# Pairing f tiles and joining outputs with scores in the steady part of an attention and feed-forward kernel

## The chip, the cores and the metric

The kernel runs on one core of one Trainium2 chip. A core has five engines that run their own instruction queues in order and meet through semaphores: PE (TensorE, matrix products), DVE (VectorE), ACT (ScalarE), POOL (GpSimd) and SP (SyncE, which here only issues DMA transfers). PE writes its results to PSUM, which has eight banks of 128 partitions by 2 KiB. Everything else lies in SBUF. The metric is the device time of one execution in microseconds (us), as the median of several runs; less is better.

## The reference

Four batches of 768 tokens with 8 heads of 64 pass through an attention with a local window and one summary per block of 32 keys, and then through a feed-forward layer with a squared ReLU.

```python
block, window = (32, 16)
k_sum = k.reshape(B, H, nb, block, D).max(axis=3)
v_sum = v.reshape(B, H, nb, block, D).mean(axis=3)
scores_l = scale * np.matmul(q, k.transpose(0, 1, 3, 2))
mask_l = np.abs(pos[:, None] - pos[None, :]) < window
scores_s = scale * np.einsum('bhsd,bhnd->bhsn', q, k_sum) + np.log(block)
scores_all = np.concatenate([np.where(mask_l, scores_l, -1e9), scores_s], axis=-1)
a = softmax(scores_all)                      # with 1e-9 added to the sum
out = np.matmul(a, np.concatenate([v, v_sum], axis=2))
...
x = out.transpose(0, 2, 1, 3).reshape(B * S, H * D)     # 3072 x 512
h = np.maximum(x @ w_in, 0.0)                           # 3072 x 2048
return h * h @ w_out                                    # 3072 x 512
```

All arrays are 32-bit floats.

## The kernel before

The 3072 tokens are 24 token tiles of 128 (six per batch, numbered g from 0). Two token tiles make a chunk c, 12 in all; the hidden width of 2048 is 16 f tiles of 128.

The feed-forward layer works on a chunk and an f tile at a time. `ffn1(c, f)` is twelve matmuls of 128 by 128 by 256 in the reduced format float32r: four slices of the model width, each as high part of w times high part of x, low part of w times high part of x, and high part of w times low part of x. They collect in one PSUM bank, `ph`; there are three such banks. `squares(ph)` then makes h squared in two parts: ACT takes the ReLU `r` and its square `gh` (the high part), DVE multiplies `ph` by `r` in place and subtracts `gh` to get `gl` (the low part). That subtraction is the last reader of the bank. `ffn2` is six matmuls of 128 by 128 by 512 per f tile (two token tiles times gh with the high part of w, gh with the low part, gl with the high part). They collect over all 16 f tiles in the two `o_ps` banks, which `evict` copies to SBUF and stores when the chunk's last f tile is in.

The attention of one token tile g is a list of steps on the same engines. `scores` (16 matmuls with a 64 by 64 stationary operand, in plain float32, each seen as two in the trace) writes `s_ps`; `softmax` runs, per head, a masked minimum on DVE (`mask_max`) and an exponential on ACT; `inverse` (DVE) and `norm` (POOL) divide by the sums; `turn` transposes the result in 32 by 32 blocks on DVE, in three parts of four instructions; `outputs` (16 matmuls with a 128 by 64 stationary operand, again two each in the trace) writes `x_ps`; `split_x` makes the high and low part of x on ACT and DVE. Beside these go loads (`load_qk`, `load_v`, two tiles ahead), and per batch the summaries of the next batch: `load_kv`, `sum_k`, `sum_v`, `place_k`, `place_v`. The tiles `s_ps` (two banks) and `x_ps` (one bank) have one buffer each.

The order of all work is written out by hand; no scheduler moves it. For chunks 0 and 1 (token tiles 0 to 6, with the conversion of the weights among them) it is the long list of tokens in `START`. From chunk 2 on, `slot(c, f, side, last)` issues one f tile: ffn1, then the ffn2 of the f tile two places back (`BEHIND` is 2), then the side work, then the squares, and then the work in `last`. Which attention steps go into which slot is given by `steps(g)`, two lists of eleven places, and by three calls of `at`, which set the places of tile 2c + 2 against f + 3, of tile 2c + 3 against f - 5 and of tile 2c + 4 against f - 13. Work in `side` stands on DVE and ACT ahead of that f tile's squares; work in `last` behind them, and PE work in it behind the slot's ffn2. PE therefore runs ffn1 (f), ffn2 (f - 2), ffn1 (f + 1), ffn2 (f - 1) and so on, with a tile's scores or outputs between an ffn2 and the next ffn1. The tokens in START are not that regular: there runs of two or three ffn1 stand together, and runs of ffn2, and one outputs stands directly ahead of a scores.

Of the kernel before, what the change touches and what calls it, by code (L numbers as in the profile page):

```python
# [24 lines left out]
P = 128  # L25
NT = S // P
# [3 lines left out]
NF = DF // P  # L30
NC4 = DM // P
SPARE = 1
BEHIND = 2
KPAD = S + 2 * WINDOW
NK = 96 + NB
FROM_KT = 4
# [35 lines left out]
def attn_ffn_kernel(ctx: ExitStack, tc: tile.TileContext, q, k, kt, v, vt, v0, w, masks, ident, mean, out):  # L72
# [43 lines left out]
    def load_qk(g):  # L116
        load_q(g)
        load_k(g)
# [36 lines left out]
    def load_kv(b, p):  # L155
        kv[b, p] = r = room(F32, "kv")
        nc.sync.dma_start(out=r[:, 0:S], in_=kt[b, p])
        nc.sync.dma_start(out=r[:, S : 2 * S], in_=vt[b, p])
# [12 lines left out]
    def place_k(g):  # L171
        nc.vector.tensor_copy(out=k_sb[g % 2][:, 4], in_=ksum.unsqueeze(1).to_broadcast([P, 2, NPAIR, NB]))

    def place_v(g):
        dst = v_sb[g % 2][96:128]
        if g % 2 == 0:
            for a in range(4):
                nc.vector.transpose(
                    out=dst[:, 0, :].rearrange("a (p c) -> a p c", c=128)[:, :, a * 32 : a * 32 + 32],
                    in_=vsum[a * 32 : a * 32 + 32],  # L180
                )
        else:
            nc.gpsimd.tensor_copy(out=dst[:, 0, :], in_=v_sb[0][96:128, 0, :])
        nc.gpsimd.tensor_copy(out=dst[:, 1, :], in_=v_sb[0][96:128, 0, :])
# [46 lines left out]
    def scores(g, p0, p1):  # L231


        if g not in s_ps:
            s_ps[g] = ps_s.tile([P, 2, NPAIR, P], F32, name="s_ps")
        for p in range(p0, p1):
            for r, s in ((0, 0), (1, 1), (0, 1), (1, 0)):
                rs, ss = slice(r * 64, r * 64 + 64), slice(s * 64, s * 64 + 64)
                nc.tensor.matmul(  # L239
                    s_ps[g][ss, r, p, 0:NK], lhsT=q_sb[g % 2][rs, s, p, :], rhs=k_sb[g % 2][rs, :, s, p, :],  # L240
                    start=True, stop=True,
                )
# [33 lines left out]
    def softmax(g, h0, h1):  # L276

        for h in range(h0, h1):
            mask_max(g, h)
            exponentials(h)  # L280

    def inverse(half):
        nc.vector.tensor_scalar_add(sm[half], sm[half], 1.0e-9)  # L283
        nc.vector.reciprocal(sm[half], sm[half])
        del nmx[half]

    def norm(half, eng):
        e = e_sb[:, half * 4 : half * 4 + 4, 0:NK]
        eng.tensor_mul(out=e, in0=e, in1=sm[half].unsqueeze(2).to_broadcast([P, 4, NK]))  # L289
# [8 lines left out]
    def turn(g, n0, n1):  # L298

        blocks = [(i, j) for i in range(4) for j in ((0, 1, 3) if i % 2 == 0 else (1, 2, 3))]  # L300
        for i, j in blocks[n0:n1]:
            nc.vector.transpose(  # L302
                out=pT[g % 2][j * 32 : j * 32 + 32, :, i * 32 : i * 32 + 32],
                in_=e_sb[i * 32 : i * 32 + 32, :, j * 32 : j * 32 + 32],
            )
# [35 lines left out]
    def ffn1(c, f):  # L341
        ph = ps_h.tile([P, 4, P], F32, name="ph").rearrange("p a b -> p (a b)")[:, 0:CT]
        n = 0
        for cc in range(NC4):
            for w, x in ((0, xh), (1, xh), (0, xl)):
                nc.tensor.matmul(  # L346
                    ph, lhsT=w_sb[f][:, w, cc * P : (cc + 1) * P], rhs=x[c][:, cc, :], start=(n == 0), stop=(n == 3 * NC4 - 1)
                )
                n += 1
        return ph  # L350
# [7 lines left out]
        return r  # L358

    def high_square(r):  # L360
        gh = work.tile([P, CT], F32R, name="gh", tag="gh", bufs=3)
        nc.scalar.activation(gh, r, AF.Square)  # L362
        return gh

# [2 lines left out]
        nc.vector.tensor_mul(out=ph, in0=ph, in1=r)  # L367

    def low_square(ph, gh):
        gl = work.tile([P, CT], F32R, name="gl", tag="gl", bufs=3)  # L370
        nc.vector.tensor_sub(out=gl, in0=ph, in1=gh.bitcast(F32))  # L371
        return gl

    def squares(ph):
        r = relu(ph, nc.scalar)
        gh = high_square(r)
        square(ph, r)
        return gh, low_square(ph, gh)

    def ffn2(c, f, gh, gl, first, last):  # L380
        if first:
            o_ps[c] = [ps_o.tile([P, DM], F32, name="o_ps") for _ in range(TPC)]
        for tt in range(TPC):
            ts_ = slice(tt * P, (tt + 1) * P)
            n = 0
            for g_, w in ((gh, 0), (gh, 1), (gl, 0)):
                nc.tensor.matmul(  # L387
                    o_ps[c][tt], lhsT=g_[:, ts_], rhs=w_sb[f][:, w, DM:],
                    start=(first and n == 0), stop=(last and n == 2),
                )  # L390
                n += 1

    def evict(c, f, tt, eng):

        if (c, tt) in parked:
            ob = parked[c, tt]
            nc.vector.tensor_add(out=ob, in0=o_ps[c][tt], in1=ob)
        else:
            ob = work.tile([P, DM], F32, name="ob", tag="ob", bufs=4)
            copy(eng, ob, o_ps[c][tt])  # L400
        if f < NF - 1:
            parked[c, tt] = ob
        else:
            r0 = c * CT + tt * P
            nc.sync.dma_start(out=out[r0 : r0 + P, :], in_=ob)
# [4 lines left out]
    n_c = n_g // TPC  # L410
    behind = []

    def follow(c, f, gh, gl, first, last):
        ffn2(c, f, gh, gl, first, last)
        if last:
            for tt in range(TPC):
                evict(c, f, tt, nc.scalar)

    def slot(c, f, side, last):


        ph = ffn1(c, f)
        if len(behind) == BEHIND:
            follow(*behind.pop(0))
        for do in side:
            do()
        behind.append((c, f, *squares(ph), f == 0, f == NF - 1))
        for do in last:
            do()

    def steps(g):


        b, t = divmod(g, NT)
        side, last = [[] for _ in range(11)], [[] for _ in range(11)]
        if b and t < 2:
            side[6].append(lambda: place_v(g))
        if t == NT - 1 and b + 1 < B:

            side[1].append(lambda: place_k(g + 1))  # L440
            side[2].append(lambda: place_k(g + 2))
        last[0].append(lambda: scores(g, 0, NPAIR))
        if g + 2 < n_g:
            last[0].append(lambda: load_qk(g + 2))
        side[1].append(lambda: softmax(g, 0, 2))
        side[2].append(lambda: softmax(g, 2, 5))
        side[3] += [lambda: inverse(0), lambda: norm(0, nc.gpsimd), lambda: softmax(g, 5, 8)]
        side[4] += [lambda: inverse(1), lambda: norm(1, nc.gpsimd)]
        for n in range(3):
            side[5 + n].append(lambda n=n: turn(g, 4 * n, 4 * n + 4))  # L450
        last[9].append(lambda: outputs(g))
        if g + 2 < n_g:
            last[9].append(lambda: load_v(g + 2))
        side[10].append(lambda: split_x(g))
        if b and t in (3, 4) and b + 1 < B:
            p = 2 * (t - 3)
            last[0].append(lambda: load_kv(b + 1, p))
            side[4] += [lambda: sum_k(b + 1, p), lambda: sum_v(b + 1, p)]
            last[4].append(lambda: load_kv(b + 1, p + 1))
            side[8] += [lambda: sum_k(b + 1, p + 1), lambda: sum_v(b + 1, p + 1)]  # L460
        return side, last


# [86 lines left out]
    with tc.manual_schedule(engines=None):  # L550
        for token in START.split():
            what, i, j, eng = re.fullmatch(r"(L:[a-z]+|F[12]|[A-Z]+)\.?(\d*)\.?(\d*)([avp]?)", token).groups()
            i, j = int(i or 0), int(j or 0)
            if what.startswith("L:"):
                load(what[2:], i)
            else:
                begin(what, i, j, engines.get(eng))
        tiles = {g: steps(g) for g in range(6, n_g)}

        def at(side, last, g, step):  # L560

            if g in tiles and 0 <= step < 11:
                side += tiles[g][0][step]
                last += tiles[g][1][step]

        place_k(7)
        load_q(7)
        load_k(7)
        load_v(6)
        load_v(7)  # L570
        load_qk(8)
        softmax(6, 0, 5)
        behind += [(*units[i][:2], *g_of[i], False, i == 31) for i in (30, 31)]
        for c in range(2, n_c):
            for f in range(NF):
                side, last = [], []
                at(side, last, 2 * c + 2, f + 3)
                at(side, last, 2 * c + 3, f - 5)
                at(side, last, 2 * c + 4, f - 13)
                slot(c, f, side, last)  # L580
        for p in behind:
            follow(*p)


def _masks():
# [64 lines left out]
```

## Time and profile before

| | us |
|---|---|
| median of three runs | 632.94 |
| the three runs | 632.94, 629.68, 633.24 |
| the profiled execution, whole | 633.5 |
| its span, first to last instruction | 631.7 |

The profile comes from one execution. The span is what the trace covers, and the rest of the execution's time lies around it. PE was busy for 39.58 of the first 60 us, for 80.56 of the next 82.03, and for all of the 438.54 after them up to 580.57. The mean clock granted to PE over the run was 0.992 of full speed.

How to read the lines below: "busy" of an engine is the time in which at least one of its instructions ran; PEld are PE's weight loads, which run beside its matmuls. A matmul's shown length includes its way through the array, so consecutive matmuls overlap in the listing and the distance between starts says what one costs. In the chain of waits each piece is given with its start, its length up to the next piece, and the line and count of its instructions. In a timeline, equal neighbours are put into one row with their count, and square brackets hold the engine's idle time before the row and what ended it. A row of waits gives the engine, line and tile that waited, what it waited for, and the total, the number and the longest of such waits.

### The profile page before, as it was taken

The numbers are of one execution on the slowest core, as the hardware profiler recorded it, in microseconds if no ns is written. First come the engines' busy times: TensorE is split into PE (matmuls) and PEld (weight loads), VectorE is DVE, ScalarE is ACT, GpSimd is POOL, SyncE is SP. The second block draws the span as 40 slices with busy tenths as digits, with TensorE's granted clock in tenths as the row PEclk, the third lists the DMA queues.
The fourth block names the chain that finished last, engine by engine and source line by source line (L and its number), as shares of the span: only waits on it lengthen the run. The fifth ranks groups of instructions, "written<-read, shape, count | busy, mean of one in ns | idle before, by whom it ended". The sixth has DMA issues, their size and how long they took to land.

```text
span 631.7 us, 13371 instructions
## 1 busy us (share of the span) xinstructions
PE 606.1 (96%) x5216; PEld 539.2 (85%) x5216; DVE 406.5 (64%) x1232; ACT 299.6 (47%) x855; POOL 96.3 (15%) x83
## 2 busy tenths in 40 slices
PE   2689999999999999999999999999999999999997
PEld 1588888988889889889888889898898898888996
DVE  4689789778656577665665686774773674664222
ACT  2789987334434435435435335345344344442322
POOL 2545762001101101001011011011011010010000
PEclk9969999999999999999999999999999999999999
DMA  9999510462220333212202315302102210000000
GB/s 285 371 352 324 204 67 6 141 208 74 67 69 34 118 119 132 68 23 79 67 7 96 117 51 162 106 2 85 62 23 69 76 26 26 34 2 1 34 0 34
DMA packets 19855, 60.38 MB, mean 96 GB/s; under 512 B 2768, under 2 KB 2896, under 8 KB 17744
## 3 DMA queue, kind: packets, MB, share of 16 engines
q1 hardware_dynamic: 19792, 59.53, 28.3%
q8 instruction: 41, 0.67, 0.4%
q14 instruction: 22, 0.18, 0.1%
HBM read 53.23 MB, written 6.29 MB: 94 GB/s over the span
## 4 chain that ended last, share of the span: by engine, by line
PE 91%; DMA 3%; DVE 3%; ACT 2%; SPq 0%; issue 0%; POOL 0%; DVEq 0%; POOLq 0%
PE ph L346 42%; PE o_ps L387 40%; PE x_ps L315 4%; PE s_ps L239 3%; DMA q_sb<-in_q 2%; DMA mask_sb<-in_masks 1%; DVE w_sb L225 1%; PE s_ps L254 1%; PE ph L295 1%; ACT e_sb L274 0%; PE o_ps L130 0%; ACT w_sb L107 0%; ACT w_raw L210 0%; SPq L153 0%; DVE sm L283 0%
## 5 line engine op out<-in xcount | busy, mean ns | idle before, releaser
L346 PE MATMUL ph<-xh,w_sb 128*128 128x256 f32 x1536 | 280.3, 282 | 1.0 <-DVE w_sb L225 0.7
L346 PEld LDWEIGHTS ph<-xh,w_sb 128*128 128x128 f32 x1536 | 243.5, 189 | 17.2 <-issue 3.0
L387 PE MATMUL o_ps<-w_sb,gh 128*128 128x512 f32 x768 | 238.2, 391 | 0.0
L346 PE MATMUL ph<-xl,w_sb 128*128 128x256 f32 x768 | 213.9, 278 | 0.2 <-DVE xl L332 0.2
L367 DVE TENSOR_TENSOR ph<-ph,r 128x256 f32<-128x256 f32 x192 | 82.6, 431 | 121.7 <-ACT r L355 119.1
L387 PE MATMUL o_ps<-w_sb,gl 128*128 128x512 f32 x384 | 151.4, 394 | 0.9 <-DVE gl L371 0.9
L355 ACT ACTIVATE r<-ph 128x256 f32<-128x256 f32 x180 | 68.4, 380 | 175.3 <-PE ph L346 164.9
L387 PEld LDWEIGHTS o_ps<-w_sb,gh 128*128 128x128 f32 x768 | 131.3, 188 | 18.0 <-issue 0.2
L346 PEld LDWEIGHTS ph<-xl,w_sb 128*128 128x128 f32 x768 | 145.1, 189 | 0.4 <-DVE xl L332 0.4
L274 ACT ACTIVATE e_sb<-e_sb,nmx 128x120 f32<-128x120 f32 x192 | 73.9, 386 | 86.3 <-DVE nmx L266 86.1
L289 POOL TENSOR_TENSOR e_sb<-e_sb,sm 128x480 f32<-128x480 f32 x43 | 43.4, 1010 | 416.1 <-DVE nmx L266 362.5
L371 DVE TENSOR_TENSOR gl<-ph,gh 128x256 fp32r<-128x256 f32 x192 | 81.5, 425 | 27.2 <-ACT gh L362 4.6
L302 DVE STREAM_TRANSPOSE pT<-e_sb 32x256 f32<-32x256 f32 x216 | 94.2, 436 | 4.4 <-POOL e_sb L289 0.8
L362 ACT ACTIVATE gh<-r 128x256 fp32r<-128x256 f32 x192 | 80.3, 418 | 13.4 <-DVE r L357 4.2
L387 PEld LDWEIGHTS o_ps<-w_sb,gl 128*128 128x128 f32 x384 | 72.2, 188 | 15.8 <-DVE gl L371 1.3
L266 DVE CUSTOM_DVE_ANT_0 e_sb<-s_ps,mask_sb 128x120 f32<-128x120 f32 x192 | 43.9, 275 | 13.5 <-PE s_ps L239 9.8
L218 POOL TENSOR_TENSOR w_raw<-w_raw 128x1024 int32<-128x1024 int32 x16 | 34.3, 2151 | 26.9 <-ACT w_raw L210 11.0
L332 DVE TENSOR_TENSOR xl<-x_ps,xh 128x512 fp32r<-128x512 f32 x24 | 16.6, 690 | 32.3 <-ACT xh L329 32.3
L315 PEld LDWEIGHTS x_ps<-pT,v_sb 128*64 128x64 f32 x768 | 25.3, 141 | 13.4 <-issue 12.6
L274 ACT ACTIVATION_READ_ACCUMULATOR e_sb<-e_sb,nmx 128x1 f32 x192 | 36.0, 188 | 0.0
L315 PE MATMUL x_ps<-pT,v_sb 128*64 128x64 f32 x768 | 28.6, 229 | 5.6 <-issue 5.3
L329 ACT CAST xh<-x_ps 128x512 fp32r<-128x512 f32 x24 | 14.1, 586 | 28.9 <-PE x_ps L315 28.5
(46 smaller groups left out, 292.3 us busy)
## 6 DMA issues: line engine op xcount, KB each, us to landing
w_raw<-in_w SPq DMA_DIRECT2D x16, 1024.0 KB, 14.1
v_sb<-in_v SPq DMA_DIRECT2D x24, 384.0 KB, 4.2
k_sb<-in_k SPq DMA_DIRECT2D x20, 384.0 KB, 3.9
kv<-in_kt SPq DMA_DIRECT2D x16, 384.0 KB, 3.4
q_sb<-in_q SPq DMA_DIRECT2D x24, 256.0 KB, 3.3
out<-ob SPq DMA_DIRECT2D x24, 256.0 KB, 2.1
kv<-in_vt SPq DMA_DIRECT2D x12, 384.0 KB, 4.2
vn<-in_v SPq DMA_DIRECT2D x2, 768.0 KB, 11.0
```

The source lines that it names most:

```text
L218: nc.gpsimd.tensor_tensor(out=hi, in0=hi, in1=lo, op=ALU.add)
L266: nc.vector.tensor_tensor_reduce(out=e_sb[:, h, 0:NK], in0=s_ps[g][:, h % 2, h // 2, 0:NK], in1=m, scale=-scale, scalar=3.0e38, op0=ALU.ad ...
L274: nc.scalar.activation(e, e, AF.Exp, bias=nmx[half][:, i : i + 1], scale=-1.0, accum_out=sm[half][:, i : i + 1])
L289: eng.tensor_mul(out=e, in0=e, in1=sm[half].unsqueeze(2).to_broadcast([P, 4, NK]))
L302: nc.vector.transpose(out=pT[g % 2][j * 32 : j * 32 + 32, :, i * 32 : i * 32 + 32], in_=e_sb[i * 32 : i * 32 + 32, :, j * 32 : j * 32 + 32],)
L315: nc.tensor.matmul(xp[o : o + 64, h // 2, s * 64 : s * 64 + 64], lhsT=v_sb[g % 2][:, s, h * 64 : h * 64 + 64], rhs=pT[g % 2][:, h, s * 64 ...
L346: nc.tensor.matmul(ph, lhsT=w_sb[f][:, w, cc * P : (cc + 1) * P], rhs=x[c][:, cc, :], start=(n == 0), stop=(n == 3 * NC4 - 1))
L355: nc.scalar.activation(r, ph, AF.Relu)
L362: nc.scalar.activation(gh, r, AF.Square)
L367: nc.vector.tensor_mul(out=ph, in0=ph, in1=r)
L371: nc.vector.tensor_sub(out=gl, in0=ph, in1=gh.bitcast(F32))
L387: nc.tensor.matmul(o_ps[c][tt], lhsT=g_[:, ts_], rhs=w_sb[f][:, w, DM:], start=(first and n == 0), stop=(last and n == 2),)
```

## The change

The steady part is rewritten; START, the layouts and all tile shapes stay as they are. A slot now issues two f tiles: ffn1 of both, then the ffn2 of the two f tiles of the slot before (`finish`), then for each of the two its side work and its squares, then, if a chunk ended, the evictions, and then the work in `last`. `gh` and `gl` get four buffers instead of three, in START as well. The list of steps has twelve places, two per slot: scores at place 1 and outputs at place 9. The calls of `at` set the places of tile 2c + 2 against f + 6 (f + 4 in chunk 2), of 2c + 3 against f - 2 and of 2c + 4 against f - 10, so that the outputs of a tile and the scores of the next fall in the same slot. Softmax is cut 3, 3, 2 heads instead of 2, 3, 3. The next batch's summaries are loaded and reduced one at a time in tiles 2 to 5 of a batch, instead of two each in tiles 3 and 4.

```diff
+    def finish():
+
+        for p in behind:
+            ffn2(*p)
+        done = [p[:2] for p in behind if p[-1]]
+        behind.clear()
+        return done[0] if done else None
 
     def slot(c, f, side, last):
-        ph = ffn1(c, f)
-        if len(behind) == BEHIND:
-            follow(*behind.pop(0))
-        for do in side:
-            do()
-        behind.append((c, f, *squares(ph), f == 0, f == NF - 1))
+        ph = [ffn1(c, f + i) for i in range(2)]
+        done = finish()
+        for i in range(2):
+            for do in side[i]:
+                do()
+            behind.append((c, f + i, *squares(ph[i]), f + i == 0, f + i == NF - 1))
+        for tt in range(TPC if done else 0):
+            evict(*done, tt, nc.scalar)
         for do in last:
             do()
...
-        gh = work.tile([P, CT], F32R, name="gh", tag="gh", bufs=3)
+        gh = work.tile([P, CT], F32R, name="gh", tag="gh", bufs=4)
...
-        last[0].append(lambda: scores(g, 0, NPAIR))
+        last[1].append(lambda: scores(g, 0, NPAIR))
...
-        side[1].append(lambda: softmax(g, 0, 2))
-        side[2].append(lambda: softmax(g, 2, 5))
-        side[3] += [lambda: inverse(0), lambda: norm(0, nc.gpsimd), lambda: softmax(g, 5, 8)]
-        side[4] += [lambda: inverse(1), lambda: norm(1, nc.gpsimd)]
+        side[2].append(lambda: softmax(g, 0, 3))
+        side[3].append(lambda: softmax(g, 3, 6))
+        side[4] += [lambda: inverse(0), lambda: norm(0, nc.gpsimd), lambda: softmax(g, 6, 8)]
+        side[5] += [lambda: inverse(1), lambda: norm(1, nc.gpsimd)]
         for n in range(3):
-            side[5 + n].append(lambda n=n: turn(g, 4 * n, 4 * n + 4))
+            side[6 + n].append(lambda n=n: turn(g, 4 * n, 4 * n + 4))
         last[9].append(lambda: outputs(g))
...
+        if b and t >= 2 and b + 1 < B:
+            last[1].append(lambda: load_kv(b + 1, t - 2))
+            side[4].append(lambda: sum_k(b + 1, t - 2))
+            side[5].append(lambda: sum_v(b + 1, t - 2))
...
-        softmax(6, 0, 5)
+        softmax(6, 0, 6)
...
-            for f in range(NF):
-                side, last = [], []
-                at(side, last, 2 * c + 2, f + 3)
-                at(side, last, 2 * c + 3, f - 5)
-                at(side, last, 2 * c + 4, f - 13)
+            for f in range(0, NF, 2):
+                side, last = [[], []], []
+                at(side, last, 2 * c + 2, f + (4 if c == 2 else 6))
+                at(side, last, 2 * c + 3, f - 2)
+                at(side, last, 2 * c + 4, f - 10)
                 slot(c, f, side, last)
```

On PE, the place of token tile 11's outputs in chunk 4. The names are those of the section on the kernel: `x_ps` rows are outputs, `s_ps` rows scores, `ph` rows ffn1, `o_ps` rows ffn2; 16 instructions in one row are all of one tile. Before, the following tile's scores stand one f tile earlier than these outputs:

```order
L387 MATMUL o_ps<-w_sb,gh 128x512 x2
L387 MATMUL o_ps<-w_sb,gl 128x512
L239 MATMUL s_ps<-k_sb_79,q_sb_83 64x120 x16
L346 MATMUL ph<-xh,w_sb 128x256 x2
L346 MATMUL ph<-xl,w_sb 128x256
```

and the outputs themselves:

```order
L387 MATMUL o_ps<-w_sb,gl 128x512
L315 MATMUL x_ps<-pT_87,v_sb_82 64x64 x16
L346 MATMUL ph<-xh,w_sb 128x256 x2
L346 MATMUL ph<-xl,w_sb 128x256
L346 MATMUL ph<-xh,w_sb 128x256 x2
```

In the changed kernel PE has, at the same outputs (its lines are one lower):

```order
L345 MATMUL ph<-xl,w_sb 128x256
L386 MATMUL o_ps<-w_sb,gh 128x512 x2
L386 MATMUL o_ps<-w_sb,gl 128x512
L386 MATMUL o_ps<-w_sb,gh 128x512 x2
L386 MATMUL o_ps<-w_sb,gl 128x512
L386 MATMUL o_ps<-w_sb,gh 128x512 x2
L386 MATMUL o_ps<-w_sb,gl 128x512
L386 MATMUL o_ps<-w_sb,gh 128x512 x2
L386 MATMUL o_ps<-w_sb,gl 128x512
L314 MATMUL x_ps<-pT_87,v_sb_82 64x64 x16
L238 MATMUL s_ps<-k_sb_79,q_sb_83 64x120 x16
L345 MATMUL ph<-xh,w_sb 128x256 x2
```

The ffn2 rows of two f tiles now follow each other, and the scores have moved behind the outputs with nothing between them. In the whole steady part this meeting occurs 16 times; tile 7's scores and tile 6's and 23's outputs stand alone.

On ACT, one tile's softmax with the split of the tile before it. Here `e_sb` rows are the exponentials of so many heads, `r` and `gh` the squares of one f tile, `xh` the split. Before:

```order
L274 ACTIVATE e_sb,sm<-e_sb,nmx 128x120 x2
L355 ACTIVATE r<-ph 128x256
L362 ACTIVATE gh<-r 128x256
L329 CAST xh<-x_ps 128x4x128
L274 ACTIVATE e_sb,sm<-e_sb,nmx 128x120 x3
L355 ACTIVATE r<-ph 128x256
L362 ACTIVATE gh<-r 128x256
L274 ACTIVATE e_sb,sm<-e_sb,nmx 128x120 x3
```

In the changed kernel:

```order
L328 CAST xh<-x_ps 128x4x128
L273 ACTIVATE e_sb,sm<-e_sb,nmx 128x120 x3
L354 ACTIVATE r<-ph 128x256
L361 ACTIVATE gh<-r 128x256
L273 ACTIVATE e_sb,sm<-e_sb,nmx 128x120 x3
L354 ACTIVATE r<-ph 128x256
L361 ACTIVATE gh<-r 128x256
L273 ACTIVATE e_sb,sm<-e_sb,nmx 128x120 x2
```

The split has moved ahead of all of the tile's exponentials. The first six heads and two squares now belong to one slot, the last two heads to the next.

More of the change, by code (lines that the diff above doesn't have):

```diff
@@ L32 @@
 SPARE = 1
-BEHIND = 2
 KPAD = S + 2 * WINDOW
@@ L369, in low_square @@
     def low_square(ph, gh):
-        gl = work.tile([P, CT], F32R, name="gl", tag="gl", bufs=3)
+        gl = work.tile([P, CT], F32R, name="gl", tag="gl", bufs=4)
         nc.vector.tensor_sub(out=gl, in0=ph, in1=gh.bitcast(F32))
@@ L411, in attn_ffn_kernel @@
     behind = []
[L413 to L417, printed above, removed]
-    def slot(c, f, side, last):
-        ph = ffn1(c, f)
-        if len(behind) == BEHIND:
-            follow(*behind.pop(0))
-        for do in side:
-            do()
-        behind.append((c, f, *squares(ph), f == 0, f == NF - 1))
+    def finish():
[4 more added lines that the diff above has]
+        return done[0] if done else None
+    def slot(c, f, side, last):
+        ph = [ffn1(c, f + i) for i in range(2)]
[6 more added lines that the diff above has]
+            evict(*done, tt, nc.scalar)
         for do in last:
@@ L434, in steps @@
         b, t = divmod(g, NT)
-        side, last = [[] for _ in range(11)], [[] for _ in range(11)]
+        side, last = [[] for _ in range(12)], [[] for _ in range(12)]
+        last[1].append(lambda: scores(g, 0, NPAIR))
+        if g + 2 < n_g:
+            last[1].append(lambda: load_qk(g + 2))
         if b and t < 2:
[L437 to L441, printed above, removed]
-        last[0].append(lambda: scores(g, 0, NPAIR))
-        if g + 2 < n_g:
-            last[0].append(lambda: load_qk(g + 2))
-        side[1].append(lambda: softmax(g, 0, 2))
-        side[2].append(lambda: softmax(g, 2, 5))
-        side[3] += [lambda: inverse(0), lambda: norm(0, nc.gpsimd), lambda: softmax(g, 5, 8)]
-        side[4] += [lambda: inverse(1), lambda: norm(1, nc.gpsimd)]
+            side[7].append(lambda: place_v(g))
+        side[2].append(lambda: softmax(g, 0, 3))
+        side[3].append(lambda: softmax(g, 3, 6))
+        side[4] += [lambda: inverse(0), lambda: norm(0, nc.gpsimd), lambda: softmax(g, 6, 8)]
+        side[5] += [lambda: inverse(1), lambda: norm(1, nc.gpsimd)]
         for n in range(3):
-            side[5 + n].append(lambda n=n: turn(g, 4 * n, 4 * n + 4))
+            side[6 + n].append(lambda n=n: turn(g, 4 * n, 4 * n + 4))
         last[9].append(lambda: outputs(g))
@@ L454, in steps @@
         side[10].append(lambda: split_x(g))
[L455 to L460, printed above, removed]
+        if b and t >= 2 and b + 1 < B:
+            last[1].append(lambda: load_kv(b + 1, t - 2))
+            side[4].append(lambda: sum_k(b + 1, t - 2))
+            side[5].append(lambda: sum_v(b + 1, t - 2))
+        if t == NT - 1 and b + 1 < B:
+            side[5] += [lambda: place_k(g + 1), lambda: place_k(g + 2)]
         return side, last
@@ L560, in at @@
         def at(side, last, g, step):
-            if g in tiles and 0 <= step < 11:
-                side += tiles[g][0][step]
-                last += tiles[g][1][step]
+            for i in range(2):
+                if g in tiles and 0 <= step + i < 12:
+                    side[i] += tiles[g][0][step + i]
+                    last += tiles[g][1][step + i]
         place_k(7)
@@ L571, in attn_ffn_kernel @@
         load_qk(8)
-        softmax(6, 0, 5)
+        softmax(6, 0, 6)
         behind += [(*units[i][:2], *g_of[i], False, i == 31) for i in (30, 31)]
         for c in range(2, n_c):
-            for f in range(NF):
-                side, last = [], []
-                at(side, last, 2 * c + 2, f + 3)
-                at(side, last, 2 * c + 3, f - 5)
-                at(side, last, 2 * c + 4, f - 13)
+            for f in range(0, NF, 2):
[3 more added lines that the diff above has]
+                at(side, last, 2 * c + 4, f - 10)
                 slot(c, f, side, last)
-        for p in behind:
-            follow(*p)
+        done = finish()
+        for tt in range(TPC):
+            evict(*done, tt, nc.scalar)
 def _masks():
```

## The prediction

> **What bounds the kernel now.** Short names: F1 and F2 are the twelve and six matmuls of one f tile (ffn1, ffn2), S and O the scores and outputs of one token tile, a chunk two token tiles. I read the head of the page first, then the busy times by stretch, the chain of waits, and the timelines of the engines. The page's engine line and the row for the stretch from the first F2 of chunk 2 to 580.57 us (PE, weight loads, DVE, ACT, POOL, with instruction counts; then clock, DMA share, GB/s):
>
> ```profile
> span 631.7 us, 13371 instructions
> PE 606.1 (96%) x5216; PEld 539.2 (85%) x5216; DVE 406.5 (64%) x1232; ACT 299.6 (47%) x855; POOL 96.3 (15%) x83
> 142.03:580.57 438.54, 438.54 (x3701) 389.68 (x3700) 285.77 (x913) 189.35 (x606) 40.86 (x45) 1.00 0.20 65
> ```
>
> In the part that is rewritten PE is busy for all of 438.54 us at full granted clock. No wait can be removed there. What can change is how tightly matmuls follow each other, and that is read off starts. The chain of waits around one S and one O (start, length to the next piece, what):
>
> ```profile
> 303.15 1.38 PE o_ps L387 x6
> 304.53 0.98 PE s_ps L239 x32
> 305.51 1.58 PE ph L346 x12
> 307.09 1.38 PE o_ps L387 x6
> 308.46 1.08 PE x_ps L315 x32
> 309.55 1.58 PE ph L346 x12
> 311.12 1.37 PE o_ps L387 x6
> 312.49 1.39 PE ph L346 x12
> ```
>
> An undisturbed f tile is 1.37 + 1.39 = 2.76 us (the last two pieces). With S it is 307.09 - 303.15 = 3.94, so S costs 1.18; with O 311.12 - 307.09 = 4.03, so O costs 1.27. Both exceed their own 0.98 and 1.08, because the F1 behind them reads 1.58 instead of 1.39.
>
> **The change, part by part.** PE's matmuls are the same in number and shape; only their order differs. F1 and F2 come in pairs in 80 slots (10 chunks of 16 f tiles). The start list already runs such pairs and triples in this trace:
>
> ```profile
> 117.51 2.75 PE ph L346 x24
> 120.26 2.75 PE o_ps L387 x12
> ...
> 128.50 4.11 PE ph L346 x36
> 132.61 4.12 PE o_ps L387 x18
> ```
>
> Two F1 in a row take 2.75 and three 4.11, so each one after the first takes 1.36 instead of 1.39. F2 doesn't care: 2.75 for two, 4.12 for three, 1.37 each. So a pair saves 0.02 to 0.03 us. I take 0.025, the middle; 80 x 0.025 = 2.0 us, ends 1.6 and 2.4.
>
> The Trainium skill has a rule against this term: "TensorE: Matmul & The Clock Gate", Part 3, The mechanism, says that a weight load overlaps a running matmul only when their row groups differ. F1 and F2 both use all 128 rows, so by it every load would be exposed whatever stands ahead, pairing would give 0 and the forecast would be 631.3. In the row of the stretch above, loads and matmuls together (389.68 + 438.54) exceed the stretch, so here they do overlap.
>
> O meets S in 16 places: the order has 17 such neighbours, and one of them (tile 5 with tile 6) is the start list's, unchanged. What is spent at the edges is in PE's timeline. In steady state, S, then O, each between an F2 and an F1:
>
> ```profile
> 304.13 0.40 PE L387 MATMUL o_ps<-w_sb,gl 128*128 128x512 f32 x1
> 304.46 1.05 PE L239 MATMUL s_ps<-k_sb,q_sb 64*64 64x120 f32 x32
> 305.44 0.51 PE L346 MATMUL ph<-xh,w_sb 128*128 128x256 f32 x2
> 305.79 0.28 PE L346 MATMUL ph<-xl,w_sb 128*128 128x256 f32 x1
> ...
> 308.07 0.40 PE L387 MATMUL o_ps<-w_sb,gl 128*128 128x512 f32 x1
> 308.39 1.15 PE L315 MATMUL x_ps<-pT,v_sb 128*64 128x64 f32 x32
> 309.48 0.50 PE L346 MATMUL ph<-xh,w_sb 128*128 128x256 f32 x2
> ...
> 312.10 0.39 PE L387 MATMUL o_ps<-w_sb,gl 128*128 128x512 f32 x1
> 312.33 0.40 PE L346 MATMUL ph<-xh,w_sb 128*128 128x256 f32 x2
> 312.56 0.28 PE L346 MATMUL ph<-xl,w_sb 128*128 128x256 f32 x1
> ```
>
> An F2's last matmul is followed after 0.23 us by F1 (312.10 to 312.33), but after 0.33 or 0.32 by S or O: entering costs 0.10. The first two F1 matmuls take 0.23 there, but 0.35 after S: leaving costs about 0.11. Now the one place where O stands directly ahead of S:
>
> ```profile
> 137.95 1.25 PE L315 MATMUL x_ps<-pT,v_sb 128*64 128x64 f32 x32 [0.35 <-DVE pT L107]
> 139.12 1.05 PE L239 MATMUL s_ps<-k_sb,q_sb 64*64 64x120 f32 x32
> 140.11 0.50 PE L346 MATMUL ph<-xh,w_sb 128*128 128x256 f32 x2
> ```
>
> O to S takes 1.17 where O to F1 takes 1.09 (308.39 to 309.48), and S to F1 0.99 where it takes 0.98. So meeting removes one entry and one exit (0.21) and puts 0.09 in their place: 0.12 by edges. Edges count a little too much, for 0.10 + 0.98 + 0.11 = 1.19 stands for S's 1.18 and 0.09 + 1.09 + 0.11 = 1.29 for O's 1.27. The two together make 0.09 + 1.17 + 0.99 + 0.11 = 2.36, less such 0.01, against 1.18 + 1.27 = 2.45: 0.10. I take 0.10, since whole costs count every matmul; 16 x 0.10 = 1.6 us. The ends are 0 (the step eats both) and 0.21 (it costs nothing): 0 to 3.4 us.
>
> Order on the other engines costs nothing as long as results are in time, so I price the cover. Three ph banks serve F1. A slot lasts 2.75 + 2.75 = 5.50 us, and the second F1 of the next slot, 5.50 + 1.39 = 6.89 after this slot's start, needs the bank of this slot's first tile: its gl must be done (the wait in question). F2 needs the second tile's gl at 5.50 + 2.75 + 1.37 = 9.62. The heaviest slot has the split of x, three heads, squares, three heads, squares. ACT and DVE rows of just these pieces, one f tile each, in the trace of before:
>
> ```profile
> 211.49 0.59 ACT L329 CAST xh<-x_ps 128x512 fp32r<-128x512 f32 x1 [1.63 <-PE x_ps L315]
> ...
> 212.71 0.27 DVE L266 CUSTOM_DVE_ANT_0 e_sb<-s_ps,mask_sb 128x120 f32<-128x120 f32 x1
> ...
> 215.11 0.43 DVE L371 TENSOR_TENSOR gl<-ph,gh 128x256 fp32r<-128x256 f32 x1
> ...
> 218.15 0.42 DVE L371 TENSOR_TENSOR gl<-ph,gh 128x256 fp32r<-128x256 f32 x1
> ```
>
> Split and xl take 1.22 (211.49 to 212.71), heads to gl 2.83 (to 215.54), then inverse and heads to the next gl 3.03 (to 218.57). O ends 0.99 ahead of the slot, since S stands behind it, so the first gl is done at -0.99 + 1.22 + 2.83 = 3.1 and the second at 6.1: 3.8 and 3.5 us early. The slots after it bring two heads with the kv sums, then turns:
>
> ```profile
> 218.78 0.92 DVE L161 TENSOR_REDUCE ksum<-kv 128x24 f32<-128x768 f32 x1
> ...
> 220.68 0.42 DVE L367 TENSOR_TENSOR ph<-ph,r 128x256 f32<-128x256 f32 x1
> ...
> 221.58 1.77 DVE L302 STREAM_TRANSPOSE pT<-e_sb 32x256 f32<-32x256 f32 x4
> ```
>
> The kv sums take 1.90 (218.78 to 220.68), squares on DVE 0.90 (to 221.58), a turn 1.8. The second slot starts with 0.6 us left over; heads (at most 3.03) and squares bring its first gl to 3.6, and the sums let it end about 0.7 late. The third holds turn, squares, turn, squares, 5.4 us, and hands on 0.6, or 1.9 where v is placed too (1.26, below). The fourth begins with the turn that O waits for: done at 0.6 + 1.8 = 2.4, or 3.7, due at 5.5. Its squares make the first gl 3.3, or 4.6, due at 6.89. Nothing is late. The moved evictions wait on ACT behind both squares, but F2's last result comes only as that slot ends, and the next F2 that needs those banks starts 2.75 later against 1.27 of copying:
>
> ```profile
> 627.37 1.27 ACT L107 COPY ob<-o_ps 128x512 f32<-128x512 f32 x2 [2.60 <-PE o_ps L387]
> ```
>
> SP issues the same transfers; each load keeps 11 us (two slots) or more to its first reader. The end keeps its F2, eviction and store.
>
> The narrow place is the beginning of chunk 2, where tiles 6 and 7 run behind the start list:
>
> ```profile
> 145.45 0.42 DVE L371 TENSOR_TENSOR gl<-ph,gh 128x256 fp32r<-128x256 f32 x1
> ...
> 148.55 1.78 DVE L302 STREAM_TRANSPOSE pT<-e_sb 32x256 f32<-32x256 f32 x4 [0.34 <-POOL e_sb L289]
> ...
> 151.35 1.26 DVE L178 STREAM_TRANSPOSE v_sb<-vsum 32x128 f32<-32x128 f32 x4
> ```
>
> The first gl (145.87) comes as before, since eight heads stand ahead of it either way; it is due at 142.03 + 1.36 + 2.75 + 1.39 = 147.53. Laid end to end from there (turns 1.78 three times, placing v 1.26, squares 0.9), the queue's tightest point is the gl of f = 6, about 0.4 us early by my estimate. A lateness there is paid once, not per slot: 0 to 2 us, taken as 0.
>
> Last, gh and gl get a fourth buffer, in the start list too. Its one PE wait for gl that this could shorten:
>
> ```profile
> PE o_ps L387 <- DVE gl L371: 0.9, 1, 0.9
> ```
>
> I take 0 (it waits for data, which a free buffer brings earlier only if ACT stood still for it), ends 0 and 0.9.
>
> Sum: 2.0 + 1.6 = 3.6 us. The profiled execution took 633.5 us (its span 631.7), giving 629.9. The median of the three runs is 632.94, 0.6 lower, so I forecast 629.3.
>
> **Rivals.**
> 1. Meeting O and S saves entry and exit whole: 16 x 0.11 = 1.8 more, 627.5. Against it stands the 1.17 of the one place seen. On this the Trainium skill, "TensorEngine Tiling (Array Packing)", Key Properties, says that a change of tiling mode drains the engine. O (128 by 64) and S (64 by 64) differ in mode, so by that rule one drain of four goes, which is what the rows give. Chance 0.08.
> 2. PE streams alike in any order: each weight load stands exposed alike, so pairs give nothing, or each change of shape costs alike, so meetings give nothing; 632.94 - 1.6 to - 2.0, about 631.1. Against it stand the start list's rows of pairs and triples. Chance 0.14. The weight-load rule above is the first of these two cases.
> 3. Chunk 2 begins late: one wait of 1 to 2 us for a ph bank, 630.3 to 631.3. For it speaks the 0.4 us of margin. Chance 0.14.
> 4. The other side: two softmax pieces in one slot hold up gl, so that the second F1 of every slot behind a softmax slot waits for its ph bank. It starts once the first gl comes more than 6.89 us after the slot's start, where rows give 3.1 to 4.6. With two such slots in each of 18 tiles, 36 waits, each 0.1 us late costs 3.6, just the gain; 1 us late gives 632.94 - 3.6 + 36 = 665. Against it: 2.3 to 3.8 us of margin and DVE at 64%. Chance 0.06.
> 5. More than counted, by over 1%: pairs at 2.4, meetings at 3.4 and the gl wait of 0.9 together are 6.7, 626.2. Chance 0.05.
>
> **How the numbers follow.** The forecast itself has 0.53. About 1% (6.3 us) is what a measurement of this kernel can tell from no change; its three runs alone span 629.68 to 633.24. The forecast and rivals 1 to 3 lie within it: 0.89. Faster by over 1% is rival 5, 0.05; slower rival 4, 0.06. The low end is rival 5's 626.2, rounded to 626. The high end takes pairs at 1.6, meetings at 0 and a wait of 2 at the start: 632.94 + 0.4 = 633.3, rounded to 633.5. That leaves out rival 4 and the far part of 5 and of the runs' own spread.
>
> **What would show it.** In the profile of after: pieces of 24 F1 matmuls at 2.75 and 12 F2 at 2.75; O to S 1.17, S to F1 0.98 with S's and O's neighbours costing about 2.35 together; PE without a gap from chunk 2 on. A row in which PE's ph waits for DVE's gl in steady state would make rivals 3 or 4 right; O to S near 1.09 rival 1; 2.78 for a pair rival 2.

## The result, and the profile after

The changed kernel takes 626.66 us (median of 8 runs, 624.4 to 629.27), where the kernel before takes 632.57 (8 runs, 629.68 to 634.09). The ratio is 0.9916, with a 95% interval from 0.9891 to 0.9941. That is 5.9 us less in the medians and 5.3 us by the ratio, with 3.7 to 6.9 by its interval. The forecast was 629.3 in a range of 626 to 633.5, so the direction and the range held, and the gain was about one and a half times the 3.6 us of the sum.

The profiled execution of the changed kernel took 625.83 us, 7.67 less than the 633.5 of before. Head of its page, and the row of busy time by stretch from 1.1 us behind chunk 2's first F1 matmul to nearly the end (PE, weight loads, DVE, ACT, POOL, with counts; then clock, DMA share, GB/s):

```profile
span 624.0 us, 13376 instructions
PE 600.9 (96%) x5216; PEld 538.4 (86%) x5216; DVE 406.6 (65%) x1232; ACT 298.4 (48%) x855; POOL 96.3 (15%) x83
138.97:620.00 481.03, 481.03 (x4009) 431.99 (x4007) 300.73 (x954) 203.53 (x645) 40.87 (x45) 1.00 0.19 61
```

PE still has no gap there. The only one since chunk 2's first F1 matmul lies just ahead of this stretch: 0.16 us at 138.51, for the low part of x, which before has too (0.16 at 140.77). So no wait was removed in the steady part and none was added. The same matmuls stand closer together. To see by how much, take the steady part from chunk 2's first F1 to the kernel's last F2 matmul. Its first row in before is the one at 140.11 us quoted in the prediction. Its last row in before, from PE's timeline:

```profile
627.63 0.40 PE L387 MATMUL o_ps<-w_sb,gl 128*128 128x512 f32 x1
```

And its first and last row in after:

```profile
137.85 0.50 PE L345 MATMUL ph<-xh,w_sb 128*128 128x256 f32 x2
...
619.93 0.40 PE L386 MATMUL o_ps<-w_sb,gl 128*128 128x512 f32 x1
```

Before it lasts 627.63 - 140.11 = 487.52 us, after it 619.93 - 137.85 = 482.08: 5.44 us less. The rest of the profiled difference, 140.11 - 137.85 = 2.26 us, lies ahead of it, in the start list, and it belongs to the execution and not to the change. In the first experiment below, whose start list is the changed kernel's, chunk 2 begins as late as before:

```profile
140.53 0.50 PE L345 MATMUL ph<-xh,w_sb 128*128 128x256 f32 x2
```

What varies are waits at the beginning of the start list: in PE's rows of waits, those of scores for `q_sb` and for `nmx` and one ahead of outputs sum to 18.7 us before and 16.4 after, 2.3 apart, and to 19.4 in that first experiment.

Where the 5.44 us come from stands in the chain of waits of after (start, length up to the next piece, what):

```profile
171.21 2.75 PE o_ps L386 x12
173.96 1.08 PE x_ps L314 x32
175.05 0.98 PE s_ps L238 x32
176.03 2.92 PE ph L345 x24
178.95 2.75 PE o_ps L386 x12
181.69 2.75 PE ph L345 x24
...
192.68 2.75 PE ph L345 x24
```

Between 181.69 and 192.68 lie two plain slots. A plain slot is (192.68 - 181.69) / 2 = 5.495 us against 2 x 2.76 = 5.52, so a pair saves 0.025 as forecast, and 80 pairs 2.0 us. A slot with a meeting runs from one F2 pair to the next, 178.95 - 171.21 = 7.74; less 5.495 it is 2.245 us for outputs and scores together, where they cost 1.18 + 1.27 = 2.45 apart. So a meeting saves 0.205, not 0.10, and 16 of them 3.3 us. Together 5.3 of the 5.44; the rest, under 0.2 us over 80 slots, is below what the rows resolve.

### The profile page after: what moved, and what is told of

It reads as the page before. It is cut to its first block, busy times and chain, and to the rows that moved or that the text cites. A ratio compares the mean times of both kernels' runs of the same rounds, so it can differ in the third digit from the quotient of the medians.

```text
span 624.0 us, 13376 instructions
## 1 busy us (share of the span) xinstructions
PE 600.9 (96%) x5216; PEld 538.4 (86%) x5216; DVE 406.6 (65%) x1232; ACT 298.4 (48%) x855; POOL 96.3 (15%) x83
## 4 chain that ended last, share of the span: by engine, by line
PE 92%; DVE 3%; DMA 2%; ACT 2%; SPq 0%; issue 0%; POOL 0%; DVEq 0%; POOLq 0%
PE ph L345 42%; PE o_ps L386 41%; PE x_ps L314 4%; PE s_ps L238 3%; DMA q_sb<-in_q 1%; DMA mask_sb<-in_masks 1%; DVE w_sb L224 1%; PE s_ps L253 1%; PE ph L294 1%; ACT e_sb L273 0%; PE o_ps L129 0%; ACT w_sb L106 0%; ACT w_raw L209 0%; SPq L152 0%; DVE sm L282 0%
## 5 line engine op out<-in xcount | busy, mean ns | idle before, releaser
L345 PE MATMUL ph<-xh,w_sb 128*128 128x256 f32 x1536 | 272.8, 280 | 0.9 <-DVE w_sb L224 0.7
L345 PEld LDWEIGHTS ph<-xh,w_sb 128*128 128x128 f32 x1536 | 238.5, 189 | 10.7 <-issue 2.9
L386 PEld LDWEIGHTS o_ps<-w_sb,gh 128*128 128x128 f32 x768 | 137.1, 188 | 24.9 <-issue 0.2
```

What stands on the lines that cost most here:

```text
L345: nc.tensor.matmul(ph, lhsT=w_sb[f][:, w, cc * P : (cc + 1) * P], rhs=x[c][:, cc, :], start=(n == 0), stop=(n == 3 * NC4 - 1))
L386: nc.tensor.matmul(o_ps[c][tt], lhsT=g_[:, ts_], rhs=w_sb[f][:, w, DM:], start=(first and n == 0), stop=(last and n == 2),)
```

## The experiments

Theory A after this reading: the step from outputs to scores costs nothing, so a meeting saves one whole entry and one whole exit, 0.21 us, and a pair 0.025. Rival B: a meeting saves 0.10 as forecast, and pairs save the rest. The first two kernels separate the two halves of the change.

**Pairs without meetings.** The changed kernel with outputs one slot later:

```diff
-        last[9].append(lambda: outputs(g))
+        last[11].append(lambda: outputs(g))
         if g + 2 < n_g:
-            last[9].append(lambda: load_v(g + 2))
-        side[10].append(lambda: split_x(g))
+            last[11].append(lambda: load_v(g + 2))
+        side[12].append(lambda: split_x(g))
```

(The lists and the bound in `at` grow from 12 to 14.)

> The changed kernel with each tile's outputs and its split of x one slot later, so that outputs and the next tile's scores no longer meet; f tiles still go in pairs. Theory A (the step from outputs to scores costs nothing, a meeting saves 0.21 us, a pair 0.025): slower than the changed kernel by 16 x 0.21 = 3.3 us, faster than before by 80 x 0.025 = 2.0, ratio to before 0.997. Rival B (a meeting saves 0.10 as forecast, and pairs save the rest of the 5.4 us measured in the steady part): faster than before by 3.8, ratio 0.994. In the chain of waits, outputs and scores each cost 1.27 and 1.18 again.

Measured: 630.35 us (12 runs) against 632.44 for before (23 runs on the same chip), ratio 0.9969 with an interval from 0.9957 to 0.9981. That is 2.0 us by the ratio and 1.2 to 2.7 by the interval: theory A's 2.0, and not B's 3.8. The steady part alone, which leaves out the start list's waits, says the same more sharply. Its last F2 row is

```profile
625.93 0.40 PE L386 MATMUL o_ps<-w_sb,gl 128*128 128x512 f32 x1
```

and its first the one at 140.53 shown above: 485.40 us, 2.12 less than the 487.52 of before. Its chain of waits has both costs back, each with its own slow F1 pair behind it:

```profile
173.91 2.75 PE o_ps L386 x12
176.66 0.98 PE s_ps L238 x32
177.64 2.94 PE ph L345 x24
180.57 2.75 PE o_ps L386 x12
183.32 1.08 PE x_ps L314 x32
184.41 2.94 PE ph L345 x24
187.34 2.75 PE o_ps L386 x12
```

From the F2 at 173.91 to the one at 180.57 are 6.66 us, 1.165 above a plain slot: that is what scores cost alone. To the one at 187.34 are another 6.77, 1.275 above a plain slot: that is what outputs cost alone.

**Meetings without pairs.** The kernel before with outputs one f tile earlier, so that 17 of them stand directly ahead of the next tile's scores:

```diff
-        last[9].append(lambda: outputs(g))
+        last[8].append(lambda: outputs(g))
         if g + 2 < n_g:
-            last[9].append(lambda: load_v(g + 2))
+            last[8].append(lambda: load_v(g + 2))
```

> The kernel before with each tile's outputs one f tile earlier, so that they stand directly ahead of the next tile's scores in 17 places; f tiles still go one at a time. Theory A: faster than before by 17 x 0.21 = 3.5 us, ratio 0.9945. Rival B: by 17 x 0.10 = 1.7, ratio 0.997. Rival C (single slots leave the turns too little time, so PE waits for outputs): a wait of PE for the turned probabilities appears, and the gain is eaten.

Measured: 629.03 us (6 runs), ratio 0.9939, interval 0.9919 to 0.9959. That is 3.9 us, 2.6 to 5.1: theory A's 3.5 lies inside, B's 1.7 outside. Apart from the 0.16 us for the low part of x, PE waited for nothing in the steady part, so C falls. The steady part's first and last rows:

```profile
139.01 0.50 PE L346 MATMUL ph<-xh,w_sb 128*128 128x256 f32 x2
...
623.02 0.40 PE L387 MATMUL o_ps<-w_sb,gl 128*128 128x512 f32 x1
```

It lasts 484.01 us, 3.51 less than before: 0.206 for each of the 17 meetings. Its chain of waits:

```profile
179.22 1.38 PE o_ps L387 x6
180.60 1.08 PE x_ps L315 x32
181.68 0.98 PE s_ps L239 x32
182.66 1.56 PE ph L346 x12
184.22 1.37 PE o_ps L387 x6
```

Here too the outputs ahead of the scores take 1.08 us, no more than ahead of an F1, and one slow F1 (1.56) stands behind both. In the whole times 2.0 and 3.9 add up to the change's 5.3 to 5.9 within their intervals. In the steady parts 2.12 and 16 x 0.206 make 5.4, the change's 5.44.

**Three buffers for gh and gl.** The changed kernel with this one edit taken back:

```diff
-        gh = work.tile([P, CT], F32R, name="gh", tag="gh", bufs=4)
+        gh = work.tile([P, CT], F32R, name="gh", tag="gh", bufs=3)
```

(and the same for gl)

> The changed kernel with three buffers for gh and gl, as before. Theory: the fourth buffer is only cover. With three, gh of a pair's second tile must wait for ffn2 of the tile three back, which ends 2.75 + 1.37 = 4.1 us into the slot; squares then end some 1.5 us later in light slots but still ahead of 9.6, so PE waits nowhere and the time is that of the changed kernel, within 0.5 us. Rival: ACT stands still behind that wait, exponentials pile up behind it, and PE waits for a ph bank, 0.3 us or more in each of 36 slots, 10 us slower.

Measured: 627.15 us (6 runs), ratio to before 0.9911, interval 0.9893 to 0.9929, not to be told from the changed kernel's 0.9916. The standstill of ACT is there, in the waits of ACT:

```profile
ACT gh L361 <- PE o_ps L386: 53.3, 66, 1.0
```

It stood 66 times, 53.3 us in all and at most 1.0 at once, and PE has no wait for gl in the steady part, which lasts 482.05 us against the changed kernel's 482.08. So the fourth buffer is cover that isn't needed at these margins.

**Four buffers in the kernel before.** The opposite edit, on the kernel before.

> The kernel before with four buffers for gh and gl. Theory: no more than 0.3 us from before, since in the profiles of before and after the start list's PE wait for gl is 0.9 us in both. Rival D: the fourth buffer is what brought the start part of the profiled run forward by 2.3 us, so this kernel is faster by about 2.3 us.

Measured: 631.69 us (12 runs), ratio 0.9988, interval 0.9975 to 1.0001. At most 1.6 us could be its doing, and no effect lies inside the interval; rival D's 2.3 us doesn't. Its steady part lasts 487.51 us, that of before 487.52.

**The row that misled the forecast.** The price of the step from outputs to scores was read off tile 5 and tile 6 in the start list, where outputs take 1.17 us. Two kernels ask what that 1.17 belongs to. In the first, the last transposes of START stand one ffn2 earlier:

```diff
- F2.28 SQ30 GL30v F2.29 SQ31 GL31v T5.0 T5.1 TC5.0v TC5.1a
- KT0 O5 PK6 VT0 S6.1 XH5a S6.0 XL5v
+ F2.28 SQ30 GL30v T5.0 T5.1 TC5.0v TC5.1a F2.29 SQ31 GL31v
+ KT0 O5 PK6 VT0 S6.1 XH5a S6.0 XL5v
```

> The changed kernel with the last transposes of the start list (tile 5) one ffn2 earlier, so that the outputs of tile 5, which stand directly ahead of tile 6's scores, no longer wait for the turned probabilities. Theory (the 1.17 us that these outputs take there comes from what is ahead of or beside them in the start list, not from the step to the scores): with the wait gone they take 1.08 to 1.09. Rival (the step from outputs to scores costs 0.08 in that place whatever is ahead): 1.17 again. The time as a whole is within 1 us of the changed kernel.

Measured: 625.88 us in one run. The outputs no longer wait, but the place tells nothing about the step, since the scores now wait. In PE's timeline they start 1.29 us after the outputs, and in DVE's the copy of the key summaries that they read ends at 136.60 + 0.26 = 136.86:

```profile
135.62 1.15 PE L314 MATMUL x_ps<-pT,v_sb 128*64 128x64 f32 x32
136.91 1.05 PE L238 MATMUL s_ps<-k_sb,q_sb 64*64 64x120 f32 x32
```

I had not counted that wait; this kernel decides nothing. In the second, START's last ffn2 stands between the two:

```diff
- KT0 O5 PK6 VT0 S6.1 XH5a S6.0 XL5v
+ KT0 O5 F2.29 PK6 VT0 S6.1 XH5a S6.0 XL5v
```

(with `F2.29` taken out of its place in the line above, and `SQ31 GL31v` ahead of the transposes)

> The changed kernel with the start list's last ffn2 moved between tile 5's outputs and tile 6's scores; the outputs still wait for the turned probabilities. Theory (the outputs are slow there by themselves, after a wait): they take 1.17 again although an ffn2 follows. Rival (the step to the scores cost it): 1.08 to 1.09. The time as a whole is up to 1.5 us above the changed kernel, for the outputs then wait longer.

Measured: 629.01 us in one run. PE's timeline:

```profile
137.76 1.25 PE L314 MATMUL x_ps<-pT,v_sb 128*64 128x64 f32 x32 [0.35 <-DVE pT L106]
138.94 0.73 PE L386 MATMUL o_ps<-w_sb,gh 128*128 128x512 f32 x2
```

The outputs take 138.94 - 137.76 = 1.18 us although no scores follow. An ffn2 behind outputs doesn't cost that by itself: where outputs that didn't wait stand ahead of one, they take 1.08 (the row at 57.31 in the next section). So the 1.17 belongs to these outputs, which begin after a wait, and not to the step behind them. Why they run slower there, by the wait or by the transposes ahead of them, was not tried.

**How far the cover reaches.** The prediction's rival for the other side was a late gl that holds the next slot's second F1. Two kernels move the squares later. First all eight heads ahead of the first squares:

```diff
-        side[2].append(lambda: softmax(g, 0, 3))
-        side[3].append(lambda: softmax(g, 3, 6))
-        side[4] += [lambda: inverse(0), lambda: norm(0, nc.gpsimd), lambda: softmax(g, 6, 8)]
+        if g > 6:
+            side[2].append(lambda: softmax(g, 0, 8))
+        side[4] += [lambda: inverse(0), lambda: norm(0, nc.gpsimd)]
```

(and `softmax(6, 0, 8)` ahead of chunk 2)

> The changed kernel with all eight heads of a tile's softmax ahead of the first squares of its slot, instead of three, three and two. Theory of the cover: the first gl moves from 3.2 us after the slot's start to 3.2 + 5 x 0.38 = 5.1, still 1.8 ahead of the 6.89 at which the next slot's second ffn1 needs its bank, so PE waits nowhere in the steady part and the time is that of the changed kernel within 0.5 us. Rival: the margin worked out from single-tile slots is not there, and PE waits for gl once per tile, 18 times 0.5 us or more, 9 us slower.

Measured: 627.41 us (5 runs), ratio 0.9928, interval 0.9905 to 0.9951, not to be told from the changed kernel's 0.9916. The steady part lasts 482.78 us, 0.70 more than in the changed kernel, so the theory's 0.5 is just missed. PE waited once for gl in the steady part, at the beginning of chunk 2, the part in which the prediction had seen the narrowest place:

```profile
160.10 0.50 PE L345 MATMUL ph<-xh,w_sb 128*128 128x256 f32 x2 [0.32 <-DVE gl L370]
```

Then the same with eight copies on ACT behind the heads:

```diff
+    junk = const.tile([P, 3, NK], F32, name="junk")
+
+    def hold():
+        for _ in range(8):
+            nc.scalar.copy(out=junk, in_=mask_sb)
...
-            side[2].append(lambda: softmax(g, 0, 8))
+            side[2] += [lambda: softmax(g, 0, 8), hold]
```

> The kernel with eight heads together and, behind them, eight copies on ACT into a tile that nothing reads, about 0.45 us each by my estimate from ACT's rows of 120 and 512 elements, which makes squares late on purpose for measuring. Theory of the deadline: the first gl comes at 5.1 + 3.6 = 8.7, 1.8 us past the 6.89 of the next slot's second ffn1; PE waits there for gl, 1.8 us once in each of 17 tiles, 31 us in all. If PE waits much less, ph banks are not what ties ffn1 to the squares; if it waits in 34 slots, one lateness is handed on.

Measured: 685.69 us in one run, 58 above the kernel with eight heads. The steady part's row of PE's waits, and one such wait in PE's timeline, between the first and the second F1 of the slot that follows the squares:

```profile
PE ph L345 <- DVE gl L370: 38.8, 17, 4.2
```

```profile
219.95 0.28 PE L345 MATMUL ph<-xl,w_sb 128*128 128x256 f32 x1
222.37 0.50 PE L345 MATMUL ph<-xh,w_sb 128*128 128x256 f32 x2 [2.14 <-DVE gl L370]
```

The wait is where the theory puts it, once in each of 17 tiles. The first, at the beginning of chunk 2, is 4.2 us long, the others are 2.1 to 2.5 long where 1.8 was expected: eight copies took 4.15 us in ACT's timeline, 0.52 each and not 0.45. The waits are 39 of the 58 us. The rest is PE itself, which takes longer for the same matmuls. Its steady part in the kernel with eight heads and in this one (length, then PE's busy time; the granted clock is the third number from the end):

```profile
138.76:621.50 482.74, 482.26 (x4015) 432.87 (x4012) 301.25 (x959) 201.92 (x645) 40.86 (x45) 1.00 0.19 61
139.26:679.82 540.56, 501.57 (x4016) 447.47 (x4012) 300.04 (x959) 265.71 (x781) 40.91 (x45) 0.97 0.17 54
```

PE is busy for 19.3 us more, at a granted clock of 0.97 instead of 1.00, on which the last section says more.

## Why the prediction was right, point by point

- **What bounds it.** PE without a gap, before and after; right.
- **Pairs, 2.0 us.** Right: 0.025 per pair in the rows, and 2.0 us (1.2 to 2.7) measured alone, 2.12 in the steady part. The weight-load rule, by which pairs would have given nothing, is not borne out here: in the steady part of after, too, loads and matmuls (431.99 + 481.03) exceed the stretch of 481.03 in which they ran. The prediction gave that rule more strictly than its source: in the same section (the Trainium skill, "TensorE: Matmul & The Clock Gate", Part 3, The mechanism) a load into the background weight buffer is pulled ahead of running matmuls as well. No run here shows which of the two these loads are.
- **Meetings, 1.6 us.** This term was mis-sized: 3.3 us in the rows of after, and measured alone with 17 of them 3.9 (2.6 to 5.1), 3.51 in the steady part. The step that failed is "So meeting removes one entry and one exit (0.21) and puts 0.09 in their place". It puts nothing in their place. The 0.09 came from the single pair of rows at 137.95, whose outputs had waited; with an ffn2 behind them such outputs took 1.18 as well. The weight loads show the same. In after, PE's weight loads around a meeting:

```profile
173.89 1.01 PEld L314 LDWEIGHTS x_ps<-pT,v_sb 128*64 128x64 f32 x32 [0.36 <-issue]
174.97 0.82 PEld L238 LDWEIGHTS s_ps<-k_sb,q_sb 64*64 64x64 f32 x32
175.96 0.30 PEld L345 LDWEIGHTS ph<-xh,w_sb 128*128 128x128 f32 x2 [0.16 <-issue]
```

  Loads stand idle for 0.36 us on entering from F2 and 0.16 on leaving to F1, and for 0.07 from outputs to scores (173.89 + 1.01 to 174.97). The trace of before had another pair of neighbours that would have warned, in the other order, scores ahead of outputs and no wait of PE in front. Its chain of waits:

```profile
56.33 0.98 PE s_ps L239 x32
57.31 1.08 PE x_ps L315 x32
58.39 1.60 PE o_ps L387 x6
```

  Scores take 0.98 there and outputs 1.08, as they do with an F1 behind them: the step was free in the row that I didn't read. Rival 1, which I gave 0.08, is what happened; its 3.6 + 1.8 = 5.4 us are the steady part's 5.44. So that 626.66 lies within the range, 0.7 us above its low end, is not the sum's doing: that end was taken from rival 5, which has the meetings at 3.4. The rule that stood beside rival 1 (the Trainium skill, "TensorEngine Tiling (Array Packing)", Key Properties: a change of tiling mode drains the engine) would leave a cost between outputs and scores. No run here shows one. Why this step is free, while those to and from the shapes of F1 and F2 cost about 0.10 us each, stays open.
- **Edges.** Right: entry and exit each near 0.10, seen as the 0.21 that a meeting saves.
- **Cover on ACT and DVE.** Right, and close. In the slot that begins at 175.96, the two gl of DVE's timeline:

```profile
178.77 0.42 DVE L370 TENSOR_TENSOR gl<-ph,gh 128x256 fp32r<-128x256 f32 x1
...
181.51 0.43 DVE L370 TENSOR_TENSOR gl<-ph,gh 128x256 fp32r<-128x256 f32 x1
```

  They end 3.2 and 6.0 us into the slot, where the prediction had 3.1 and 6.1. The deadline is real: the last experiment crossed it and paid at the named F1.
- **Beginning of chunk 2.** Right that nothing is late. At the place that the prediction named, the gl of f = 6 and the second F1 of the next slot (that of f = 9), DVE's and PE's timelines of after have:

```profile
162.84 0.42 DVE L370 TENSOR_TENSOR gl<-ph,gh 128x256 fp32r<-128x256 f32 x1
```

```profile
164.20 0.39 PE L345 MATMUL ph<-xh,w_sb 128*128 128x256 f32 x2
```

  That is 164.20 - 163.26 = 0.94 us early, where I had estimated 0.4. With all heads first a wait of 0.32 us came one slot earlier, since tile 7's eight heads then stand ahead of the squares of f = 4.
- **The fourth buffers.** Right at 0: neither taking them away after nor adding them before changed the time beyond its interval, and the steady parts differ by 0.03 and 0.01 us.
- **Rivals 2, 3 and 5.** Rival 2 had pairs or meetings at nothing; each of the two alone made the kernel faster. Rival 3's late beginning of chunk 2 did not come. Rival 5 had its meetings right, but neither pairs above 2.1 nor the gl wait's 0.9 came with them.
- **Rival 4, the other side.** Its mechanism exists, but in the changed kernel it doesn't start. Its count of 36 waits, two per tile, was not tried: the last experiment puts all the heads and the copies into one slot of each tile. There PE waited once per tile, 17 times, and no lateness was handed on to the slot behind.

## What to carry to other kernels

Where one engine has no gap, instructions of the same number and shape can still take less time in another order: look for places where the distance between starts is longer just behind a change of shape, count these changes, and try whether the odd shapes can stand next to each other. Here the step between the two of them was free; another pair has to be measured. Price a step from an occurrence that didn't wait, and look for every occurrence in the trace, in both orders, before one is taken as the price. And when work on other engines is moved, compute when its result is due and when it comes, in the slots' own time; here a margin of some us made a change of their order free.

## What the runs showed of the hardware

PE's clock fell after 8 of the 17 waits of the last experiment, and the fall cost time beyond the wait. Around the second of them, 2.14 us up to 194.14, PE's busy time and granted clock by stretches of 2 us (length, busy, count, clock, DMA share, GB/s):

```profile
192.00:194.00 2.00, 0.00 (x1) 1.00 0.01 5
194.00:196.00 2.00, 1.86 (x10) 0.67 0.04 8
196.00:198.00 2.00, 2.00 (x8) 0.50 0.00 0
198.00:200.00 2.00, 2.00 (x10) 0.98 0.00 0
```

After about two idle microseconds the granted clock was 0.50 of full speed for more than two busy ones. The third wait, the one up to 222.37 shown with that experiment and also 2.14 us long, was followed by full clock:

```profile
223.00:224.00 1.00, 1.00 (x10) 1.00 0.00 0
```

Over the execution the mean was 0.969, against 0.992 in the kernel with eight heads alone. Spread over the eight waits, the 19.3 us of longer busy time are about 2.4 us each (an estimate). So a wait of two microseconds in an otherwise busy PE can cost more than itself, here about as much again where the clock fell, and whether it does differs from one to the next. What decides it was not tried.
